# Attention beside a mixer on one core: which PSUM bank the value products and the output products take in each cycle

## The chip, the cores and the metric

The kernel runs on one core of a Trainium2 chip. The metric is the device time of one execution in microseconds (us). Before the change three runs gave 950.87, 950.03 and 948.76 us, with a median of 950.03 us.

## What is computed

The input `x` has 2048 tokens of 448 features, in float32. Two branches are computed and mixed token by token with a gate `g`:

```python
q = (x @ wq).reshape(B, S, 16, 28).transpose(0, 2, 1, 3)     # 16 heads of 28
k = x @ wk; v = x @ wv                                        # one head of keys and values, shared
p = softmax(einsum("bhqd,bkd->bhqk", q, k) * 28 ** -0.5)
a = einsum("bhqk,bkd->bhqd", p, v).transpose(0, 2, 1, 3).reshape(B, S, 448) @ wo
h = gelu(layernorm(x) @ w1)           # its four quarters shifted by +1, -1, +2, -2 tokens
x1 = x + shifted(h) @ w2
b = x1 + gelu(layernorm(x1) @ w3) @ w4
out = g * a + (1 - g) * b             # g = sigmoid(sum(x * gate_w))
```

## The kernel before

The program has three stages. The first (to about 125 us) makes queries, keys, values and the token mixer; the second (to about 400 us) is the mixer's MLP; the third, from about 400 us to the end, is attention with the output projection. The change lies in the third stage alone. The order of the instructions on TensorE, VectorE, ScalarE and SyncE is written out by hand; each engine runs its instructions in the order in which the code issues them, with semaphores between the engines.

The third stage goes through 16 units (`u`), one for each block of 512 tokens and each group of four heads. A unit has eight cycles (`i` from 0 to 7), so there are 128 cycles (`c`). A cycle handles two tiles of 128 keys, A and B:

- `scores` (line 203): twelve matmuls for a tile, in three rounds of four. The four heads of a round run side by side on four strips of 32 rows, each into its own PSUM bank: two single banks and the two halves of a pair.
- `exps` (line 850): ScalarE's exponentials of the scores, into an SBUF tile `p`. The two single banks are read one at a time (128x512), the pair of tile B at once (128x1024, `p<-pair`). The pair of tile A is first moved to SBUF by VectorE (line 888, `p<-pair`, COPY), and ScalarE then works on it in place (`p<-p`).
- `values` (line 861): eight products of `p` with the values, for the two tiles of the cycle before, all accumulated in one single bank (column strips of 32). VectorE adds that bank to the unit's sum `o` with `values_end` (line 787; line 785 for a unit's first cycle).
- `run_jobs`: output products of an earlier unit in halves of 224 columns (line 813 on TensorE, `wo_products`), followed by VectorE's addition to the output tile (line 832, `wo_add`; line 844 for a last part of the MLP that is done in the first cycles). Most cycles have one half, cycle `i == 5` has two, and from the fifth cycle of the last unit on each has two. In cycle `i == 2` the place is taken by `max_part` (line 210 on TensorE, a reduction of line 212 on VectorE), which serves the next unit. Six cycles, at the start of the stage and in the last unit, have nothing of the kind.

There are four single banks, `singles`. In each cycle they are named `s0, s1, s2, s3_`; in the next cycle the two halves of the list change places, so that what was `s0, s1` becomes `s2, s3_`. Tile A's first two heads go to `s0` and `s1`, tile B's to `s2` and `s3_`. When the exponentials of tile A have read `s0` and `s1`, these two take the cycle's other products: `s0` the output products, `s1` the values. In the next cycle tile B's scores go into both.

TensorE's order in a cycle is: scores A, scores B, output products, values. VectorE's is: the move of pair A, small work of the cycle (reciprocals, the normalisation, the next unit's queries), `wo_add`, `values_end`. The lines that set it:

```python
s0, s1, s2, s3_ = singles if c % 2 == 0 else singles[2:] + singles[:2]
...
run_jobs(s0, 2 if i == TWICE or (u == NU - 1 and i > 3) else 1)
...
pv = s1
values(k - 2, pv, True, False)
values(k - 1, pv, False, True)
values_end(v, pv)
```

After the last cycle comes a tail for the last unit: the last two value tiles, their addition to `o` (line 980), four transposes (line 986) into PSUM, normalisation by token (lines 947 and 951), four transposes back (line 956, `tail_back`) with ScalarE's copies (line 957), the output products of four times 128 tokens (line 813, `tail_wo`) and their additions and stores (lines 964 to 969). Between them stand a few matmuls on zeros (line 977, `keep_warm`) and the reduction of a check (lines 1000 to 1011) whose result a branch reads; the branch's other side is not taken with these inputs.

Of the kernel before, what the change touches and what calls it, by code (L numbers as in the profile page):

```python
# [16 lines left out]
P = 128  # L17
# [7 lines left out]
NT = S // P  # L25
# [16 lines left out]
def gated_mix_kernel(  # L42
# [137 lines left out]
    NU = NB * NG  # L180
# [24 lines left out]
    def max_part(u, ts, ps):  # L205
        if u not in mx_of:
            mx_of[u] = late.tile([P, 4, 4], F32, tag="mr", bufs=2, name=f"mr_{u}")
        n = len(ts)
        for i, t in enumerate(ts):
            nc.tensor.matmul(ps[:, i * 4 * MK:(i + 1) * 4 * MK], qh_of[u][:, t * P:(t + 1) * P], khd,  # L210
                             start=True, stop=True)
        nc.vector.reduce_max(mx_of[u][:, :, ts[0]:ts[0] + n].rearrange("p j t -> p t j"),
                             ps[:, 0:n * 4 * MK].rearrange("p (t j k) -> p t j k", t=n, j=4), axis=AX.X)
# [19 lines left out]
    def max_end(u):  # L233
        mr = mx_of.pop(u).rearrange("p j t -> p (j t)")
        mc = late.tile([P, 32], F32R, tag="mc", bufs=2, name=f"mc_{u}")
        nc.vector.tensor_scalar(mc[:, 0:16], mr, -1.0, None, op0=ALU.mult)
        nc.vector.scalar_tensor_tensor(mc[:, 16:32], mr, -1.0, f32(mc)[:, 0:16],
                                       op0=ALU.mult, op1=ALU.subtract)
        mrow = late.tile([P, 32], F32, tag="mrow", bufs=2, name=f"mrow_{u}")
        nc.vector.transpose(mrow, f32(mc))  # L240
        for k in range(2):
            rows = f32(qh_of[u])[DH + k:P:32, :].rearrange("j (t p q) -> p j t q", p=4, q=32)
            for p in range(4):
                nc.sync.dma_start(rows[p], mrow[32 * p + 16 * k:32 * p + 16 * k + 16, :])
# [4 lines left out]
    with tc.tile_pool(name="s1b", bufs=1) as s1b, \  # L249
            tc.tile_pool(name="ps1", bufs=1, space=PSUM) as ps1:  # L250
        s1_stack = ExitStack()
        s1 = s1_stack.enter_context(tc.tile_pool(name="s1", bufs=1))
# [491 lines left out]
    with tc.tile_pool(name="s3", bufs=1, reuse_waits="tile") as s3, \  # L744
# [4 lines left out]
        singles = [mm_tile("bank_0"), mm_tile("bank_1"), misc_tile("bank_2"), max_tile("bank_3")]  # L749
        pairs = [ps3.tile([P, 2, 512], F32, name=f"pair_{i}") for i in range(2)]  # L750
# [10 lines left out]
        def q_fetch(u):  # L761
            if u < NU:
                q_load(u, qr)

        def q_begin(u):
            q_split(u, s3.tile([P, 512], F32R, tag="qh", bufs=3, name=f"qh_{u}"),
                    s3.tile([P, 512], F32R, tag="ql", bufs=3, name=f"ql_{u}"))
# [14 lines left out]
        def values_end(u, pv):  # L782
            if u not in o_of:
                o_of[u] = s3.tile([P, 512], F32, tag="o", bufs=2, name=f"o_{u}")
                nc.vector.tensor_copy(o_of[u], pv)
            else:
                nc.vector.tensor_add(o_of[u], o_of[u], pv)  # L787
# [7 lines left out]
        def recip(u, o, rt, checked=True):  # L795
            if checked:
                check(rt.rearrange("p (a b) -> p a b", b=4), 0)
            rr = s3.tile([P, 16], F32, tag="rr", bufs=2, name=f"rr_{u}")
            nc.vector.reciprocal(rr, rt)
            rd = dram.tile([4, 512], F32, tag="rd", bufs=2, name=f"rd_{u}")  # L800
            nc.sync.dma_start(rd.rearrange("j (a b) -> (j a) b", b=16), rr)
            rb = s3.tile([P, 512], F32, tag="rb", bufs=2, name=f"rb_{u}")
            nc.sync.dma_start(rb, rd.unsqueeze(1).broadcast_to([4, 32, 512]))
            return u, o, rb

        def norm(u, o, rb):
            on_of[u] = s3.tile([P, 512], F32, tag="on", bufs=2, name=f"on_{u}")
            nc.vector.tensor_mul(on_of[u], o, rb)
# [9 lines left out]
        halves = [slice(0, D // 2), slice(D // 2, D)]  # L818
# [30 lines left out]
        def exps(p, heads, source=None):  # L849
            nc.scalar.activation(p[:, heads], p[:, heads] if source is None else source, AF.Exp, scale=SCALE)  # L850

        def score_tiles(u, kt, first, second, pair):
            scores(u, kt, [first, second, pair[:, 0], pair[:, 1]])
            p_of[u * NT + kt] = p = s3.tile([P, 4, 512], F32, tag="p", bufs=PB, name=f"p_{u}_{kt}")
            return p

        def values(k, pv, first, last):
            u, kt = divmod(k, NT)
            p = p_of.pop(k)
            for j in range(4):  # L860
                nc.tensor.matmul(pv[32 * j:32 * j + 32, :], vext[:, kt, :], p[:, j],  # L861
                                 start=first, stop=last, tile_position=(0, 32 * j))

        jobs = [(w4_products, w4_add, (t,), cols) for t in range(4) for cols in halves]
        left, right, both = slice(0, 1), slice(1, 2), slice(2, 4)
        sums, norms, later = [], [], []
        pv = None
        MAX_AT = 2
        TWICE = 5

        def run_jobs(ps, n):
            adds = []
            for _ in range(min(n, len(jobs))):
                products, add, args, cols = jobs.pop(0)
                products(*args, ps, cols)
                adds.append((add, args, cols))
            for add, args, cols in adds:
                add(*args, ps, cols)

        for c in range(NU * NT // 2 + 1):  # L880
            u, i = divmod(c, NT // 2)
            k = 2 * c
            s0, s1, s2, s3_ = singles if c % 2 == 0 else singles[2:] + singles[:2]
            if u < NU:
                pa = score_tiles(u, 2 * i, s0, s1, pairs[0])
                exps(pa, left, s0.unsqueeze(1))
                exps(pa, right, s1.unsqueeze(1))
                nc.vector.tensor_copy(pa[:, both], pairs[0])  # L888
                while later:
                    later.pop(0)()  # L890
                if i == 1 and sums:
                    norms.append(recip(*sums.pop()))
                if i == 1 and u == 0:
                    q_begin(1)
                    q_fetch(2)
                if i == 3 and norms:
                    w = norms[0][0]
                    norm(*norms.pop())
                if i == 6 and u + 2 < NU:
                    q_begin(u + 2)  # L900
                    q_fetch(u + 3)
                pb = score_tiles(u, 2 * i + 1, s2, s3_, pairs[1])
                exps(pb, left, s2.unsqueeze(1))
                exps(pb, right, s3_.unsqueeze(1))
                exps(pb, both, pairs[1])
                exps(pa, both)
                if i == 4 and u:
                    jobs += [(wo_products, wo_add, (u - 1, t), cols) for t in range(4) for cols in halves]
                if i == MAX_AT and u + 1 < NU:
                    max_part(u + 1, range(4), s0)  # L910
                    later.append(lambda u=u: max_end(u + 1))
                elif c == 0:
                    run_jobs(s0, 2)
                    run_jobs(s1, 2)
                else:
                    run_jobs(s0, 2 if i == TWICE or (u == NU - 1 and i > 3) else 1)
            if c:
                v = (c - 1) // (NT // 2)
                pv = s1
                values(k - 2, pv, True, False)  # L920
                values(k - 1, pv, False, True)
                if (v, i) != (NU - 1, 0):
                    values_end(v, pv)
                if i == 0 and v < NU - 1:
                    sums.append(sums_begin(v))
            if u == NU:
                break
        assert not sums and not norms and not jobs and not later

        u = NU - 1  # L930
# [2 lines left out]
        on = s3.tile([P, 512], F32, tag="on", bufs=2, name=f"on_{u}")  # L933
        on_of[u] = on
        toks = [slice(t * P, (t + 1) * P) for t in range(4)]
        b1, b0, b2, b3 = singles
        tp = [q.rearrange("p (t n) -> p t n", t=4) for q in (b1, b2)]
        tq = [q[:, 0:P] for q in (b3, b0, pairs[0][:, 0], pairs[1][:, 0])]
        wo_banks = [b1, b2, b3, b0]
        rr = s3.tile([P, 2, 2, 4], F32, name="rr4")  # L940
        on4 = s3.tile([P, 4, P], F32, name="on4")

# [12 lines left out]
        def tail_back(t):  # L955
            nc.tensor.transpose(tq[t], on4[:, t], ident)
            nc.scalar.copy(on[:, toks[t]], tq[t])
# [17 lines left out]
        def keep_warm(n):  # L975
            for _ in range(n):
                nc.tensor.matmul(pairs[1][:, 1, 0:256], warm[:, 0:P], warm, start=True, stop=True)
# [21 lines left out]
        worst = s3.tile([P, 1], F32, name="worst")  # L999
        nc.vector.tensor_reduce(worst, good, axis=AX.XY, op=ALU.min)  # L1000
        tail_back(2)
        keep_warm(2)
        tail_wo(0)
        tail_back(3)
        tail_wo(1)
        tw = pairs[0][0:1, 1, 0:P]
        nc.tensor.transpose(tw, worst, ident)
# [84 lines left out]
```

## Time and profile before

| | us |
|---|---|
| median of three runs | 950.03 |
| the profiled execution | 949.08 |
| its span, first to last instruction | 947.3 |
| TensorE (PE) busy | 936.6 |
| ScalarE (ACT) busy | 638.3 |
| VectorE (DVE) busy | 509.9 |
| GpSimd (POOL) busy | 80.8 |

The profile is of one execution. PE is the matmuls, PEld the loads of their stationary operand, which run ahead of the matmuls; a busy PE is not a PE at its peak, since matmuls overlap and their ends are modelled. In the lists of instructions in order of time a row gives the start, the time from the first start to the last end of the merged instructions, the engine, the line, the operation, the tile written and the tiles read, the shape, and the count; in brackets stands the engine's idle time before the row and what ended it. The granted TensorE clock is 0.998 of full speed over the span.

### The profile page before, as it was taken

How to read it: one execution, taken by the hardware profiler on the slowest of the kernel's cores; microseconds unless marked ns; L12 is line 12 of the kernel's file. 1: busy time of each engine (PE TensorE's matmuls, PEld its weight loads, DVE VectorE, ACT ScalarE, POOL GpSimd, SP SyncE). 2: the span in 40 equal slices, each digit the busy share in tenths (PEclk: the TensorE clock that was granted, in tenths of full speed). 3: DMA queues.
4: the chain of work that ended last, by engine and by line, in shares of the span. 5: the costliest groups of instructions: out<-in, count | busy, mean ns of one | idle time of the engine just before them, and what ended most of it. 6: DMA issues, size and time to landing. Idle time of an engine off the chain costs nothing.

```text
span 947.3 us, 19530 instructions
## 1 busy us (share of the span) xinstructions
PE 936.6 (99%) x8087; PEld 580.0 (61%) x8087; DVE 509.9 (54%) x830; ACT 638.3 (67%) x1006; POOL 80.8 (9%) x111
## 2 busy tenths in 40 slices
PE   9999999999999999999999999999999999999997
PEld 6788888888888888844444444444444444444442
DVE  4664464432432421265666666666666666666654
ACT  5542444322222222299999999999999999999993
POOL 3342500200000420110000000000000000000000
PEclk9999999999999999999999999999999999999999
DMA  8933452300300300010000001000010000110001
GB/s 291 303 84 76 138 167 84 94 9 1 84 1 1 84 1 1 23 38 24 12 23 14 23 32 34 24 12 23 15 50 24 14 23 12 33 44 11 6 13 43
DMA packets 40423, 47.05 MB, mean 50 GB/s; under 512 B 10120, under 2 KB 28488, under 8 KB 40328
## 3 DMA queue, kind: packets, MB, share of 16 engines
q1 hardware_dynamic: 37304, 40.27, 14.2%
q10 hardware_dynamic: 3024, 5.47, 1.6%
q8 instruction: 65, 1.06, 0.5%
q14 instruction: 30, 0.25, 0.1%
HBM read 32.56 MB, written 11.67 MB: 47 GB/s over the span
## 4 chain that ended last, share of the span: by engine, by line
PE 97%; ACT 1%; DVE 0%; DMA 0%; issue 0%; DVEq 0%
PE bank L861 24%; PE bank L203 21%; PE bank L813 7%; PE acc L682 5%; PE acc L684 5%; PE acc L683 5%; PE g L135 4%; PE g L136 4%; PE g L137 4%; PE pair L203 3%; PE hs L460 1%; PE hs L461 1%; PE g L138 1%; PE g L139 1%; PE h L135 1%; PE h L136 1%
## 5 line engine op out<-in xcount | busy, mean ns | idle before, releaser
L850 ACT ACTIVATE p<-bank 128x512 f32<-128x512 f32 x512 | 264.6, 603 | 33.0 <-PE pair L203 14.6
L861 PE MATMUL bank<-p,vext 128*32 128x512 f32 x2048 | 244.2, 593 | 1.7 <-ACT p L850 1.7
L888 DVE COPY p<-pair 128x1024 f32<-128x1024 f32 x128 | 156.7, 1224 | 23.5 <-PE pair L203 20.3
L672 ACT ACTIVATE gh<-g 128x512 fp32r<-128x512 f32 x55 | 32.9, 598 | 184.1 <-PE g L139 184.1
L203 PEld LDWEIGHTS bank<-qh,kh 32*128 32x128 f32 x512 | 70.1, 182 | 135.2 <-ACT p L850 106.0
L203 PE MATMUL bank<-qh,kh 32*128 32x512 f32 x512 | 146.4, 469 | 0.2
L850 ACT ACTIVATE p<-p 128x1024 f32<-128x1024 f32 x128 | 139.6, 1091 | 0.0
L787 DVE TENSOR_TENSOR o<-o,bank 128x512 f32<-128x512 f32 x111 | 76.3, 688 | 113.8 <-PE bank L861 96.4
L850 ACT ACTIVATE p<-pair 128x1024 f32<-128x1024 f32 x128 | 135.1, 1055 | 0.0
L203 PE MATMUL bank<-ql,kh 32*128 32x512 f32 x512 | 132.1, 395 | 0.0
L203 PE MATMUL pair<-qh,kh 32*128 32x512 f32 x512 | 128.0, 495 | 0.3 <-DVE x L738 0.3
L203 PE MATMUL bank<-qh,kl 32*128 32x512 f32 x512 | 128.2, 388 | 0.0
L674 DVE TENSOR_TENSOR gl<-gf,gh 128x512 fp32r<-128x512 f32 x55 | 38.3, 696 | 166.2 <-ACT gf L673 166.2
L861 PEld LDWEIGHTS bank<-p,vext 128*32 128x32 f32 x2048 | 57.9, 109 | 102.5 <-issue 77.1
L203 PE MATMUL pair<-qh,kl 32*128 32x512 f32 x512 | 101.2, 390 | 0.0
L203 PE MATMUL pair<-ql,kh 32*128 32x512 f32 x512 | 100.5, 387 | 0.0
L682 PE MATMUL acc<-w4h,gh 128*128 128x448 f32 x220 | 80.3, 365 | 0.0
L684 PE MATMUL acc<-w4h,gl 128*128 128x448 f32 x220 | 80.0, 364 | 0.0
L683 PE MATMUL acc<-w4l,gh 128*128 128x448 f32 x220 | 80.0, 363 | 0.0
L203 PEld LDWEIGHTS bank<-qh,kl 32*128 32x128 f32 x512 | 70.6, 183 | 7.9
L813 PE MATMUL bank<-wof,on 128*32 128x224 f32 (+1 forms) x992 | 70.2, 369 | 0.0
L135 PE MATMUL g<-ah,w3h 128*128 128x512 f32 x168 | 65.8, 392 | 0.0
(200 smaller groups left out, 1424.3 us busy)
## 6 DMA issues: line engine op xcount, KB each, us to landing
qd<-qf ACTq DMA_DIRECT2D x16, 256.0 KB
rb<-rd SPq DMA_DIRECT2D x15, 256.0 KB
x<-in_x_dram SPq DMA_DIRECT2D x4, 896.0 KB
xd<-xt SPq DMA_DIRECT2D x16, 224.0 KB
w34raw<-in_w_dram SPq DMA_DIRECT2D x7, 512.0 KB
qr<-qd SPq DMA_DIRECT2D x64, 56.0 KB
out_dram<-ot SPq DMA_DIRECT2D x15, 224.0 KB
w34raw<-in_w_dram SPq DMA_DIRECT2D x7, 448.0 KB
```

The costliest lines, as they stand in the source:

```text
L135: nc.tensor.matmul(ps, wh[:, c, :], ah[:, c, :], start=(c == 0), stop=False)
L136: nc.tensor.matmul(ps, wh[:, c, :], al[:, c, :], start=False, stop=False)
L203: nc.tensor.matmul(ps[j], k[h, keys], q[h, :], start=(r == 0), stop=(r == 2), tile_position=(32 * j, 0))
L674: nc.vector.tensor_sub(gl, gf, f32(gh))
L682: nc.tensor.matmul(ps, gh[:, tok], w4h[i][:, k, :], start=(f == 0), stop=False)
L683: nc.tensor.matmul(ps, gh[:, tok], w4l[i][:, k, :], start=False, stop=False)
L684: nc.tensor.matmul(ps, gl[:, tok], w4h[i][:, k, :], start=False, stop=(f == stop))
L787: nc.vector.tensor_add(o_of[u], o_of[u], pv)
L813: nc.tensor.matmul(ps[32 * i:32 * i + 32, :], a[:, c:c + 32], w, start=True, stop=True, tile_position=(0, 32 * i))
L850: nc.scalar.activation(p[:, heads], p[:, heads] if source is None else source, AF.Exp, scale=SCALE)
L861: nc.tensor.matmul(pv[32 * j:32 * j + 32, :], vext[:, kt, :], p[:, j], start=first, stop=last, tile_position=(0, 32 * j))
L888: nc.vector.tensor_copy(pa[:, both], pairs[0])
```

## The change

The value products now take `s0` and come directly behind scores B, with `values_end` behind them on VectorE; the output products (or `max_part`) take `s1` and come behind the values, and so do their additions on VectorE. The order of the cycle on TensorE becomes: scores A, scores B, values, output products.

In the last cycle VectorE no longer moves pair A; ScalarE reads it from PSUM as its third exponential of the cycle, ahead of tile B's. The values of the last two tiles are taken out of the loop and go into the first half of pair A instead of a single bank.

In the tail the transposes and products are spread over the four single banks in another way, the fourth transpose back comes directly behind the third, and two matmuls on zeros that stood between are gone, so that the first two output products follow one another.

```diff
-        for c in range(NU * NT // 2 + 1):
+        NC = NU * NT // 2
+        for c in range(NC):
...
+            pa = score_tiles(u, 2 * i, s0, s1, pairs[0])
+            exps(pa, left, s0.unsqueeze(1))
+            exps(pa, right, s1.unsqueeze(1))
+            if c < NC - 1:
                 nc.vector.tensor_copy(pa[:, both], pairs[0])
...
+            else:
+                exps(pa, both, pairs[0])
...
+            exps(pb, left, s2.unsqueeze(1))
+            exps(pb, right, s3_.unsqueeze(1))
+            exps(pb, both, pairs[1])
+            if c < NC - 1:
                 exps(pa, both)
...
-                    max_part(u + 1, range(4), s0)
...
-                    run_jobs(s0, 2 if i == TWICE or (u == NU - 1 and i > 3) else 1)
             if c:
                 v = (c - 1) // (NT // 2)
-                pv = s1
-                values(k - 2, pv, True, False)
-                values(k - 1, pv, False, True)
-                if (v, i) != (NU - 1, 0):
-                    values_end(v, pv)
+                values(k - 2, s0, True, False)
+                values(k - 1, s0, False, True)
+                values_end(v, s0)
...
+            if i == MAX_AT and u + 1 < NU:
+                max_part(u + 1, range(4), s1)
...
+                run_jobs(s1, 2 if i == TWICE or (u == NU - 1 and i > 3) else 1)
+        pv = pairs[0][:, 0]
+        values(2 * NC - 2, pv, True, False)
+        values(2 * NC - 1, pv, False, True)
...
-        b1, b0, b2, b3 = singles
-        tp = [q.rearrange("p (t n) -> p t n", t=4) for q in (b1, b2)]
-        tq = [q[:, 0:P] for q in (b3, b0, pairs[0][:, 0], pairs[1][:, 0])]
-        wo_banks = [b1, b2, b3, b0]
+        tp = [q.rearrange("p (t n) -> p t n", t=4) for q in singles[:2]]
+        tq = [singles[2 + t % 2][:, t // 2 * P:t // 2 * P + P] for t in range(4)]
+        wo_banks = singles
...
         tail_back(2)
-        keep_warm(2)
+        tail_back(3)
         tail_wo(0)
-        tail_back(3)
         tail_wo(1)
```

More of the change, by code (lines that the diff above doesn't have):

```diff
@@ L883, in gated_mix_kernel @@
             s0, s1, s2, s3_ = singles if c % 2 == 0 else singles[2:] + singles[:2]
[L884 to L887, printed above, removed]
+            pa = score_tiles(u, 2 * i, s0, s1, pairs[0])
+            exps(pa, left, s0.unsqueeze(1))
+            exps(pa, right, s1.unsqueeze(1))
+            if c < NC - 1:
                 nc.vector.tensor_copy(pa[:, both], pairs[0])
[L889 to L905, printed above, removed]
-                exps(pa, both)
-                if i == 4 and u:
-                    jobs += [(wo_products, wo_add, (u - 1, t), cols) for t in range(4) for cols in halves]
-                if i == MAX_AT and u + 1 < NU:
-                    max_part(u + 1, range(4), s0)
[L911 to L915, printed above, removed]
-                    run_jobs(s0, 2 if i == TWICE or (u == NU - 1 and i > 3) else 1)
@@ new lines, in gated_mix_kernel @@
+            else:
+                exps(pa, both, pairs[0])
+            while later:
+                later.pop(0)()
+            if i == 1 and sums:
+                norms.append(recip(*sums.pop()))
+            if i == 1 and u == 0:
+                q_begin(1)
+                q_fetch(2)
+            if i == 3 and norms:
+                w = norms[0][0]
+                norm(*norms.pop())
+            if i == 6 and u + 2 < NU:
+                q_begin(u + 2)
+                q_fetch(u + 3)
+            pb = score_tiles(u, 2 * i + 1, s2, s3_, pairs[1])
@@ L924, in gated_mix_kernel @@
                 if i == 0 and v < NU - 1:
                     sums.append(sums_begin(v))
-            if u == NU:
-                break
+            if i == 4 and u:
+                jobs += [(wo_products, wo_add, (u - 1, t), cols) for t in range(4) for cols in halves]
+            if i == MAX_AT and u + 1 < NU:
+                max_part(u + 1, range(4), s1)
+                later.append(lambda u=u: max_end(u + 1))
+            elif c == 0:
+                run_jobs(s0, 2)
+                run_jobs(s1, 2)
+            else:
+                run_jobs(s1, 2 if i == TWICE or (u == NU - 1 and i > 3) else 1)
```

## The prediction

> **What bounds the kernel now.** I read the page first, then the waits inside the attention stage (440 to 930 us), then single cycles in order of time, engine by engine.
>
> ```profile
> PE 936.6 (99%) x8087; PEld 580.0 (61%) x8087; DVE 509.9 (54%) x830; ACT 638.3 (67%) x1006; POOL 80.8 (9%) x111
> ...
> L850 ACT ACTIVATE p<-bank 128x512 f32<-128x512 f32 x512 | 264.6, 603 | 33.0 <-PE pair L203 14.6
> ```
> ```profile
> PEld bank L203 <- DVE o L787: 19.7, 103, 0.5
> ```
>
> TensorE is never without work, so a gain must come out of its own stream. The wait that the change touches is that of the score loads for VectorE's sum (L787): 103 times, 19.7 us in all, 0.19 each. A cycle with one output product shows what it does. These are the weight loads, then VectorE, then ScalarE:
>
> ```profile
> 893.95 0.18 PEld L203 LDWEIGHTS bank<-qh,kh 32*128 32x128 f32 x1 [0.18 <-DVE o L787]
> ...
> 894.85 0.16 PEld L813 LDWEIGHTS bank<-wof,on 128*32 128x32 f32 x8 [0.36 <-ACT p L850]
> ...
> 897.08 0.18 PEld L203 LDWEIGHTS bank<-qh,kh 32*128 32x128 f32 x2 [0.84 <-ACT p L850]
> ...
> 897.65 0.18 PEld L203 LDWEIGHTS bank<-qh,kh 32*128 32x128 f32 x1
> 898.02 0.18 PEld L203 LDWEIGHTS bank<-qh,kh 32*128 32x128 f32 x1 [0.18 <-DVE o L787]
> ```
> ```profile
> 895.57 0.45 DVE L832 SCALAR_TENSOR_TENSOR ot<-bank,gg,ot 128x224 f32<-128x224 f32 x1 [0.27 <-PE bank L813]
> 897.28 0.69 DVE L787 TENSOR_TENSOR o<-o,bank 128x512 f32<-128x512 f32 x1 [1.25 <-PE bank L861]
> ```
> ```profile
> 894.06 2.07 ACT L850 ACTIVATE p<-bank 128x512 f32<-128x512 f32 x4
> ```
>
> Tile B's first load stands at 897.65. Its second, for the bank that the values had, waits until L787 ends at 897.97 and comes at 898.02, 0.05 behind it. From that held load to the first product load is 0.90 us (893.95 to 894.85), and from there to the next held load 3.17 us: 4.07 us, the cycle. So a cycle is the loop "products, VectorE reads the last bank, scores B, products". ScalarE is not in it yet: the first of four exponentials takes 0.60 (603 ns in the page's row) and starts at 894.06, so it would let the product loads go at about 894.71, 0.14 before they do. More than 0.14 us per cycle can't be won here.
>
> **One product, 88 cycles.** The change turns the order round. What values alone take is seen in a cycle without products:
>
> ```profile
> 433.24 0.18 PEld L203 LDWEIGHTS bank<-qh,kh 32*128 32x128 f32 x1 [0.18 <-DVE o L787]
> ...
> 434.50 0.16 PEld L861 LDWEIGHTS bank<-p,vext 128*32 128x32 f32 x8 [0.73 <-ACT p L850]
> ...
> 436.35 0.18 PEld L203 LDWEIGHTS bank<-qh,kh 32*128 32x128 f32 x2 [0.84 <-ACT p L850]
> ...
> 437.29 0.18 PEld L203 LDWEIGHTS bank<-qh,kh 32*128 32x128 f32 x1 [0.17 <-DVE o L787]
> ```
> ```profile
> 436.55 0.69 DVE L787 TENSOR_TENSOR o<-o,bank 128x512 f32<-128x512 f32 x1 [1.95 <-PE bank L861]
> ```
>
> From the first load of the values to the next scores 1.85 us, and the sum starts 2.05 us after that first load, 0.20 behind the score load. Laid on the cycle above: values loaded at 894.85, sum from 896.90 to 897.59, which is 0.38 earlier than before. The product adds 0.38 us behind the values (2.23 from 894.85 to 897.08, less 1.85), so the next scores still load at 897.08, and with the same lag of 0.20 VectorE may have the product at 897.28. It is then still at the sum: the addition L832, which stood ahead of the sum, is now queued behind it, and tile B's second load waits for the addition. What an addition costs directly behind a long operation shows elsewhere:
>
> ```profile
> 592.86 0.69 DVE L195 TENSOR_TENSOR ql<-qr,qh 128x512 fp32r<-128x512 f32 x1
> 593.47 0.44 DVE L832 SCALAR_TENSOR_TENSOR ot<-bank,gg,x 128x224 f32<-128x224 f32 x1
> ```
> ```profile
> 572.31 0.36 DVE L832 SCALAR_TENSOR_TENSOR ot<-bank,gg,ot 128x224 f32<-128x224 f32 x1
> ```
>
> L832 starts 0.08 before the end of the operation ahead of it (593.55) and takes 0.44; behind a reciprocal of 16 elements it took 0.36. With the first row, which has an operation of the sum's kind and size ahead, it runs from 897.51 to 897.95 and the load comes at 898.00: 0.02 earlier than before, 88 times, 1.8 us gained. Bounds: with 0.36 it is 0.10 earlier (8.8 us gained), without the overlap 0.06 later (5.3 us lost). I take 0.02.
>
> The Trainium skill's page "VectorE: DVE Perf Modes", section "The DRAIN you can't avoid", speaks against this change: the next operation does not start until the pipe of the one before is empty. By that rule the sum would come out at the lossy end; the two rows at 592.86 and 593.47 show an earlier start, so I give the measurement the greater weight.
>
> **Two products, 17 cycles that have a cycle behind them** (the fifth-index cycle of 15 units, and two more of the last).
>
> ```profile
> 587.58 0.54 PEld L813 LDWEIGHTS bank<-wof,on 128*32 128x32 f32 x16 [0.36 <-ACT p L850]
> ...
> 590.19 0.18 PEld L203 LDWEIGHTS bank<-qh,kh 32*128 32x128 f32 x2 [0.84 <-ACT p L850]
> ...
> 591.13 0.18 PEld L203 LDWEIGHTS bank<-qh,kh 32*128 32x128 f32 x1 [0.18 <-DVE o L787]
> ```
> ```profile
> 588.68 0.81 DVE L832 SCALAR_TENSOR_TENSOR ot<-bank,gg,x 128x224 f32<-128x224 f32 x2 [0.65 <-PE bank L813]
> ```
>
> The first addition starts 1.10 us behind the first product load, so it waits for both products. Now the sum runs from 589.63 to 590.32, the products are ready at 590.19 + 0.20 = 590.39, and VectorE stands idle for 0.07 before them. The two additions end at 591.20, the load comes at 591.25 instead of 591.13. That is 0.12 later; as the lag of 0.20 was read behind values, I take 0.13: 17 x 0.13 = 2.2 us lost.
>
> **The next unit's maximum, 15 cycles.**
>
> ```profile
> 575.16 0.52 PEld L210 LDWEIGHTS bank<-khd,qh 128*128 128x128 f32 x4 [0.36 <-ACT p L850]
> ...
> 577.61 0.18 PEld L203 LDWEIGHTS bank<-qh,kh 32*128 32x128 f32 x2 [0.84 <-ACT p L850]
> ...
> 578.54 0.18 PEld L203 LDWEIGHTS bank<-qh,kh 32*128 32x128 f32 x1 [0.18 <-DVE o L787]
> ```
> ```profile
> 575.93 0.69 DVE L212 TENSOR_REDUCE mr<-bank 128x16 f32<-128x512 f32 x1 [0.33 <-ACT p L850]
> ```
>
> The sum would run from 577.21 to 577.90, the reduction (ready at 577.81) from 577.82 to 578.51, the load at 578.56: 0.02 later, 0.3 us lost in all.
>
> **No product, 6 cycles.** Here the values start at 434.50 because they wait for the second exponential's bank; the loop would let them go 0.90 behind 433.24, at 434.14, so the first bank saves 0.36 us, and nothing is written into the second, so the following scores are not held at all. What is late next is ScalarE:
>
> ```profile
> 403.73 1.09 ACT L850 ACTIVATE p<-p 128x1024 f32<-128x1024 f32 x1
> 404.68 2.10 ACT L850 ACTIVATE p<-bank 128x512 f32<-128x512 f32 x4
> 406.59 1.11 ACT L850 ACTIVATE p<-pair 128x1024 f32<-128x1024 f32 x1
> 407.49 1.14 ACT L850 ACTIVATE p<-p 128x1024 f32<-128x1024 f32 x1
> ```
>
> Its steps here are 0.95, 1.91 and 0.90, 3.76 us in all against a cycle of 4.05 (433.24 to 437.29). A saving between 0.29 and 0.36, and a little more in the cycles behind: 6 x 0.33 = 2.0 us gained (1.7 to 2.2).
>
> **The last cycle and the tail.**
>
> ```profile
> 928.49 0.54 PEld L813 LDWEIGHTS bank<-wof,on 128*32 128x32 f32 x16 [0.36 <-ACT p L850]
> ...
> 931.69 0.28 PEld L861 LDWEIGHTS bank<-p,vext 128*32 128x32 f32 x8 [0.58 <-ACT p L850]
> ...
> 936.31 0.16 PEld L813 LDWEIGHTS bank<-wof,on 128*32 128x32 f32 x8 [0.21 <-issue]
> 937.20 0.14 PEld L956 LDWEIGHTS pair<-ident,on 128*128 128x128 f32 x1 [0.73 <-issue]
> 937.46 0.16 PEld L813 LDWEIGHTS bank<-wof,on 128*32 128x32 f32 x8
> ```
> ```profile
> 933.70 0.88 DVE L980 TENSOR_TENSOR oo<-o,bank 128x128 f32<-128x128 f32 x4 [1.72 <-PE bank L861]
> ```
>
> Before, the last products waited 0.58 us at 931.69 for ScalarE's very last exponential, tile A's. Now that one is third and tile B's last one ends at about the same time, but only half of one of the last two tiles needs it. TensorE then runs through: values and two products take 2.61 us (587.58 to 590.19) with a change of tile shape at their end, so the last values load near 931.0 and VectorE's L980 starts at 931.0 + 2.05 = 933.0 instead of 933.70: 0.7 us gained. VectorE's move in that cycle was beside other work and saves nothing itself. In the tail the two output products no longer have a transpose (0.26 us, 937.20 to 937.46) and its two changes of shape between them; the fourth transpose now waits for VectorE ahead of the first product, about where the two dropped matmuls ran. I take 0.3 us (0.1 to 0.4).
>
> **The sum.** -1.8 + 2.2 + 0.3 - 2.0 - 0.7 - 0.3 = -2.3 us on an execution of 949.08 us (span 947.3), which gives 946.8. That execution lies 0.95 us under the median of 950.03; on the median's scale the forecast is **947.7 us**, 0.24% less. About 0.2% (1.9 us) is what a measurement of this kernel tells from no change.
>
> **The rivals.**
>
> *VectorE's operations don't overlap (slower).* Place: the addition behind the sum, in the 88 cycles with one product and the 15 with a maximum. Each loses the 0.08: +0.06 x 88 = 5.3 and +0.10 x 15 = 1.5, with 2.2 for two products and -3.0 for the rest: +6.0, 956.0 us. It decides from 0.05 us on: (2.3 + 1.9) / 88. For it speaks that no row of before shows an addition behind L787; against it the row at 593.47. Chance 0.12. The page's rule named above is this rival.
>
> *The addition is short (faster).* If it takes 0.36 behind the sum, 88 x 0.08 = 7.0 us more are gained: 940.7 us. Only a very short operation stood ahead of it where it was so. Chance 0.10.
>
> *The cycles without products don't shrink.* If ScalarE, or the move of pair A behind it, sets those six cycles already, 2.0 us are missing: 949.7 us, no change. Its rows leave 0.29 us per cycle, so chance 0.10.
>
> **How the numbers follow.** The forecast has the remaining 0.68. It lies 0.4 us past the bound of 1.9, and an error of 0.01 us per cycle moves it by about 1, so I give 0.40 of it to faster and 0.28 to no change. Faster 0.40 + 0.10 = 0.50, same 0.28 + 0.10 = 0.38, slower 0.12. The range from 943.0 to 952.5 leaves out the far ends of the first two rivals, about 0.1 on either side.
>
> **What would show it.** Right: the score loads now wait for L832 and no longer for L787, with about the same sum (near 20 us) in the waits; from the first load behind the scores to the next held load 3.15 us with one product (3.17 now) and 3.68 with two (3.55 now, 587.58 to 591.13), and the cycles without any at 3.8; L980's idle time behind TensorE, and the 0.58 us at the last values, gone. Wrong: waits of the score loads well under 15 us or over 25 us, additions that start at or behind the end of L787, or a stretch of 3.55 as before in the cycles with two products.

## The result, and the profile after

The changed kernel took 947.22 us (median of 12 runs, 946.89 to 948.89) and the kernel before 949.54 us (median of 12 runs beside it, 948.76 to 950.88). The ratio is 0.9976, with a 95% interval of 0.9967 to 0.9985: 2.3 us faster, where 2.3 had been forecast. The difference is small and the agreement of the totals says little by itself, so the steps are looked at one by one.

The page, then a row of the waits between 440 and 930 us:

```profile
span 945.1 us, 19526 instructions
...
PE 936.3 (99%) x8085; PEld 585.7 (62%) x8085; DVE 504.1 (53%) x829; ACT 637.3 (67%) x1006; POOL 80.8 (9%) x111
```
```profile
PEld bank L203 <- DVE ot L832: 19.6, 99, 0.3
```

TensorE's busy time is nearly what it was. The wait for the sum (L787, 19.7 us, 103 times) is replaced by a wait for the addition (L832, 19.6 us, 99 times); behind a maximum the loads now wait for the reduction L212 (2.6 us, 14 times). The wait has changed its name and about kept its size.

**One product.** Weight loads of the changed kernel in order of time, then VectorE (start, duration, then the idle time ahead of the row and what ended it):

```profile
893.67 0.16 PEld L861 LDWEIGHTS bank<-p,vext 128*32 128x32 f32 x8 [0.36 <-ACT p L850]
...
894.98 0.13 PEld L813 LDWEIGHTS bank<-wof,on 128*32 128x32 f32 x4 [0.30 <-ACT p L850]
...
895.90 0.19 PEld L203 LDWEIGHTS bank<-qh,kh 32*128 32x128 f32 x2 [0.36 <-ACT p L850]
...
896.82 0.18 PEld L203 LDWEIGHTS bank<-qh,kh 32*128 32x128 f32 x1
...
897.71 0.16 PEld L861 LDWEIGHTS bank<-p,vext 128*32 128x32 f32 x8 [0.37 <-ACT p L850]
```
```profile
895.72 0.69 DVE L787 TENSOR_TENSOR o<-o,bank 128x512 f32<-128x512 f32 x1 [1.57 <-PE bank L861]
896.32 0.44 DVE L832 SCALAR_TENSOR_TENSOR ot<-bank,gg,ot 128x224 f32<-128x224 f32 x1
```

The sum starts 2.05 us behind the first load of the values and ends at 896.41. The addition starts 0.09 before that, ends at 896.76, and the held load comes at 896.82 (its idle time is 0.15 us, too short for the view to print). From the first load behind the scores to the held load it is 3.15 us, as forecast.

**Two products.** The same views of the cycle with two, and the held load of the cycle behind it:

```profile
585.81 0.16 PEld L861 LDWEIGHTS bank<-p,vext 128*32 128x32 f32 x8 [0.36 <-ACT p L850]
...
588.42 0.18 PEld L203 LDWEIGHTS bank<-qh,kh 32*128 32x128 f32 x2 [0.36 <-ACT p L850]
...
589.49 0.18 PEld L203 LDWEIGHTS bank<-qh,kh 32*128 32x128 f32 x1 [0.31 <-DVE ot L832]
...
593.56 0.18 PEld L203 LDWEIGHTS bank<-qh,kh 32*128 32x128 f32 x1 [0.18 <-DVE ot L832]
```
```profile
587.86 0.69 DVE L787 TENSOR_TENSOR o<-o,bank 128x512 f32<-128x512 f32 x1 [1.56 <-PE bank L861]
588.63 0.81 DVE L832 SCALAR_TENSOR_TENSOR ot<-bank,gg,x 128x224 f32<-128x224 f32 x2
```

VectorE is idle for 0.08 between the end of the sum (588.55) and the additions, which wait for the products. The held load comes 3.68 behind the first one; before it was 3.55. The cycle behind it, from 589.49 to 593.56, takes the usual 4.07.

**The next unit's maximum.** Weight loads, then VectorE:

```profile
573.42 0.16 PEld L861 LDWEIGHTS bank<-p,vext 128*32 128x32 f32 x8 [0.38 <-ACT p L850]
...
576.81 0.18 PEld L203 LDWEIGHTS bank<-qh,kh 32*128 32x128 f32 x1 [0.18 <-DVE mr L212]
```
```profile
575.47 0.69 DVE L787 TENSOR_TENSOR o<-o,bank 128x512 f32<-128x512 f32 x1 [1.59 <-PE bank L861]
576.07 0.68 DVE L212 TENSOR_REDUCE mr<-bank 128x16 f32<-128x512 f32 x1
```

3.39 us, where it was 3.38 (575.16 to 578.54).

**No product.** Weight loads, VectorE and ScalarE:

```profile
432.23 0.18 PEld L203 LDWEIGHTS bank<-qh,kh 32*128 32x128 f32 x2 [0.40 <-DVE o L787]
...
433.24 0.16 PEld L861 LDWEIGHTS bank<-p,vext 128*32 128x32 f32 x8 [0.47 <-ACT p L850]
...
436.03 0.18 PEld L203 LDWEIGHTS bank<-qh,kh 32*128 32x128 f32 x2 [0.40 <-DVE o L787]
```
```profile
435.29 0.69 DVE L787 TENSOR_TENSOR o<-o,bank 128x512 f32<-128x512 f32 x1 [1.71 <-PE bank L861]
```
```profile
432.51 2.15 ACT L850 ACTIVATE p<-bank 128x512 f32<-128x512 f32 x4
434.42 1.16 ACT L850 ACTIVATE p<-pair 128x1024 f32<-128x1024 f32 x1
435.33 1.20 ACT L850 ACTIVATE p<-p 128x1024 f32<-128x1024 f32 x1
436.27 2.20 ACT L850 ACTIVATE p<-bank 128x512 f32<-128x512 f32 x4
```

The cycle takes 3.80 us instead of 4.05. ScalarE starts each step before the recorded end of the one ahead; its steps of 1.91, 0.91 and 0.94 make 3.76 of the 3.80.

**The last cycle and the tail.** The last held load, the last values, the last sum, and the last transposes back with the first products behind them; the last held load of the kernel before stands at the end:

```profile
926.40 0.18 PEld L203 LDWEIGHTS bank<-qh,kh 32*128 32x128 f32 x1 [0.31 <-DVE ot L832]
...
929.62 0.32 PEld L861 LDWEIGHTS pair<-p,vext 128*32 128x32 f32 x8
...
934.08 0.33 PEld L958 LDWEIGHTS bank<-ident,on 128*128 128x128 f32 x2 [0.24 <-ACT on L959]
934.54 0.16 PEld L813 LDWEIGHTS bank<-wof,on 128*32 128x32 f32 x8
```
```profile
931.83 0.88 DVE L982 TENSOR_TENSOR oo<-o,pair 128x128 f32<-128x128 f32 x4 [0.89 <-issue]
```
```profile
927.59 0.18 PEld L203 LDWEIGHTS bank<-qh,kh 32*128 32x128 f32 x1 [0.18 <-DVE o L787]
```

The row at 929.62 shows no idle time: the 0.58 us ahead of the last values is gone. The idle time of VectorE ahead of the last sum (L980 before, L982 now) is not gone, as the prediction's sign had it, but fell from 1.72 to 0.89.

### The profile page after: what moved, and what is told of

It reads as the page before. It is cut to its first block, busy times and chain, and to the rows that moved or that the text cites. A ratio compares the mean times of both kernels' runs of the same rounds, so it can differ in the third digit from the quotient of the medians.

```text
span 945.1 us, 19526 instructions
## 1 busy us (share of the span) xinstructions
PE 936.3 (99%) x8085; PEld 585.7 (62%) x8085; DVE 504.1 (53%) x829; ACT 637.3 (67%) x1006; POOL 80.8 (9%) x111
## 4 chain that ended last, share of the span: by engine, by line
PE 97%; ACT 1%; DMA 0%; DVE 0%; issue 0%; DVEq 0%
PE bank L861 24%; PE bank L203 22%; PE bank L813 5%; PE acc L682 5%; PE acc L684 5%; PE acc L683 5%; PE g L135 4%; PE g L136 4%; PE g L137 4%; PE pair L203 3%; PE hs L460 1%; PE hs L461 1%; PE g L138 1%; PE g L139 1%; ACT p L850 1%; PE h L135 1%
## 5 line engine op out<-in xcount | busy, mean ns | idle before, releaser
L787 DVE TENSOR_TENSOR o<-o,bank 128x512 f32<-128x512 f32 x111 | 76.3, 687 | 149.0 <-PE bank L861 135.1
L861 PEld LDWEIGHTS bank<-p,vext 128*32 128x32 f32 x2032 | 53.0, 109 | 122.5 <-issue 76.0
L813 PEld LDWEIGHTS bank<-wof,on 128*32 128x32 f32 x992 | 32.0, 110 | 64.4 <-issue 32.1
L813 PE MATMUL bank<-wof,on 128*32 128x224 f32 (+1 forms) x992 | 67.5, 359 | 0.0
```

The lines of the kernel that those rows point to most:

```text
L813: nc.tensor.matmul(ps[32 * i:32 * i + 32, :], a[:, c:c + 32], w, start=True, stop=True, tile_position=(0, 32 * i))
```

## The experiments

Theory A is that of the prediction: in nearly all cycles the stream is held by VectorE's two operations in a row, sum and addition, whichever comes first, so exchanging them brings next to nothing; what is gained comes from the cycles without products and from the end. Its test is to make one of these operations short. The other theories stand in the expectations. The cycle lengths below are taken from one move of pair A to the next and stand in the order `i` = 0 to 7, for a unit without a disturbed cycle.

**The loop's order alone** (`loop_only`; last cycle and tail as before):

```diff
-            if c < NC - 1:
-                nc.vector.tensor_copy(pa[:, both], pairs[0])
-            else:
-                exps(pa, both, pairs[0])
+            nc.vector.tensor_copy(pa[:, both], pairs[0])
...
-            if c < NC - 1:
-                exps(pa, both)
+            exps(pa, both)
...
-        pv = pairs[0][:, 0]
+        pv = singles[1]
...
```

> The loop's new order alone; last cycle and tail as before. Theory A (VectorE's last read of the two banks sets the cycle; what the values gain by coming first is given back by the addition queued behind them, two-product cycles lose, only the six cycles without products gain): 1.0 to 1.6 us faster than before, with 6 x 0.33 gained and 16 or 17 x 0.13 lost inside. Rival B (all cycles gain a little because the new order suits TensorE): nearly the whole 2.3 us, and no cycle longer than before. Rival C (the gain sits in the last cycle and the tail): no change.

Measured: 948.32 us, ratio 0.9988 (0.9979 to 0.9997), 1.2 us faster.

**The last cycle and the tail alone** (`ends_only`; the loop's order as before):

```diff
-            if c:
...
-                values(k - 2, s0, True, False)
...
-                max_part(u + 1, range(4), s1)
+                max_part(u + 1, range(4), s0)
...
-                run_jobs(s1, 2 if i == TWICE or (u == NU - 1 and i > 3) else 1)
+                run_jobs(s0, 2 if i == TWICE or (u == NU - 1 and i > 3) else 1)
+            if c:
...
+                values(k - 2, s1, True, False)
...
```

> The new last cycle and tail alone; the loop in its order of before. Theory A: 1.0 us faster than before (0.7 in the last cycle, 0.3 in the tail). Rival B: 0 to 0.3 us. Rival C: 2.3 us.

Measured: 948.49 us, ratio 0.9986 (0.9977 to 0.9995), 1.05 us faster. The two parts add up to the whole: half of the gain comes from one cycle in 128 and the tail.

**Two products ahead of the values** (`mixed`), beside **the changed kernel again** (`after_again`):

```diff
+            two = len(jobs) > 1 and c and (i == TWICE or (u == NU - 1 and i > 3))
+            pv = s0
+            if two:
+                run_jobs(s0, 2)
+                pv = s1
             if c:
...
-                values(k - 2, s0, True, False)
...
+                values(k - 2, pv, True, False)
+                values(k - 1, pv, False, True)
...
+            elif not two:
+                run_jobs(s1, 1)
```

> As the changed kernel, but in the 18 cycles with two products these come ahead of the values and take the first bank, as before. Theory A: the loss of 0.13 to 0.14 us in 17 of them goes, so 2.2 us faster than the changed kernel, 4.5 us faster than before. Rival B: 17 of 128 cycles lose their share of the gain, 0.3 us slower than the changed kernel.

> The changed kernel, on the same chip as the parts: 2.3 us faster than before.

Measured: `mixed` 945.70 us, ratio 0.9956 (0.9942 to 0.9969); `after_again` 947.52 us, 0.9977 (0.9968 to 0.9987). Putting the old order back where there are two products is worth 1.8 us, where 2.2 were expected. Counted from move to move it shows in the cycle behind: 4.06 us instead of 4.19 in the median. The moves at the two ends of such a cycle, in `mixed` and in the changed kernel:

```profile
590.05 1.23 DVE L889 COPY p<-pair 128x1024 f32<-128x1024 f32 x1 [0.19 <-PE pair L203]
...
594.12 1.22 DVE L889 COPY p<-pair 128x1024 f32<-128x1024 f32 x1 [0.19 <-PE pair L203]
```
```profile
589.50 1.23 DVE L889 COPY p<-pair 128x1024 f32<-128x1024 f32 x1
...
593.69 1.22 DVE L889 COPY p<-pair 128x1024 f32<-128x1024 f32 x1 [0.18 <-PE pair L203]
```

**Short additions** (`short_add`). The additions leave out most columns, each reads `x1` instead of the running tile, and `x1` is what is stored:

```diff
-            before = x1[:, n, :] if g == 0 else ot_of[n]
+            before = x1[:, n, :]
...
-            nc.vector.scalar_tensor_tensor(ot_of[n][:, cols], ps[:, cols], gg[:, n:n + 1], before[:, cols],
+            few = slice(cols.start, cols.start + 8)
+            nc.vector.scalar_tensor_tensor(ot_of[n][:, few], ps[:, few], gg[:, n:n + 1], before[:, few],
...
-                nc.sync.dma_start(out[0, n * P:(n + 1) * P, :], ot_of[n])
+                nc.sync.dma_start(out[0, n * P:(n + 1) * P, :], x1[:, n, :])
```

> The changed kernel, with the loop's additions of the output products cut from 224 to 8 columns (the other columns are left out, and the tiles stored are not the sums). TensorE does the same work. Theory A: the addition then ends about 0.25 us earlier, before tile B's scores want the bank, so no score load is held in cycles with one product, and the first exponential becomes the limit at about 3.93 us in place of 4.06: 88 x 0.12 = 10.6 us, and with two products some 16 x 0.25 = 4 us: 12 to 15 us faster than the changed kernel, 933 to 936 us. Rival D (VectorE's reads don't set the cycle; drains between tile shapes or the exponentials do): within 1 us of the changed kernel.

Measured: 933.88 us, ratio 0.9836 (0.9821 to 0.9852). TensorE has the same work, and the time is in the range that was expected (933 to 936). Rows of a cycle:

```profile
895.52 0.30 PEld L203 LDWEIGHTS bank<-qh,kh 32*128 32x128 f32 x2
...
896.65 0.16 PEld L862 LDWEIGHTS bank<-p,vext 128*32 128x32 f32 x8 [0.47 <-ACT p L851]
```
```profile
894.76 0.69 DVE L787 TENSOR_TENSOR o<-o,bank 128x512 f32<-128x512 f32 x1 [1.46 <-PE bank L862]
895.37 0.22 DVE L833 SCALAR_TENSOR_TENSOR ot<-bank,gg,x 128x8 f32<-128x8 f32 x1
```

The addition is done at 895.59, and both score loads of tile B's round come together, at 895.52 and 895.64. A cycle with one product takes 3.94 us instead of 4.05. The next bound stands at 896.65: the values wait for the first exponential. This agrees with theory A: the length of the addition is on the path.

**Short sums in the order of before** (`short_sum`):

```diff
-                nc.vector.tensor_add(o_of[u], o_of[u], pv)
+                nc.vector.tensor_add(o_of[u][:, 0:8], o_of[u][:, 0:8], pv[:, 0:8])
```

> The kernel before, with the sum of the values cut to 8 of 512 columns in seven of a unit's eight cycles (the other columns are left out). Theory A: the order before was held by the sum, so it gains what the changed kernel gains from a short addition: 112 x 0.12 = 13 us, 935 to 938 us. Rival D: no change.

Measured: 945.28 us, ratio 0.9957 (0.9942 to 0.9972): 4 us faster where 13 were expected, a miss. A cycle with one product went from 4.07 to 4.05 only, and one with two from 4.45 to 4.31: some 0.02 x 88 and 0.15 x 17, which makes the 4 us. Rows of a cycle with one:

```profile
894.51 0.16 PEld L813 LDWEIGHTS bank<-wof,on 128*32 128x32 f32 x8 [0.47 <-ACT p L850]
895.00 0.16 PEld L861 LDWEIGHTS bank<-p,vext 128*32 128x32 f32 x8 [0.33 <-ACT p L850]
...
896.86 0.18 PEld L203 LDWEIGHTS bank<-qh,kh 32*128 32x128 f32 x2 [0.84 <-ACT p L850]
...
897.43 0.19 PEld L203 LDWEIGHTS bank<-qh,kh 32*128 32x128 f32 x2
```
```profile
897.05 0.16 DVE L787 TENSOR_TENSOR o<-o,bank 128x8 f32<-128x8 f32 x1 [1.36 <-PE bank L861]
```

The sum ends at 897.21 and the hold is gone: both loads come at 897.43. But with the product ahead the values go into the second bank, and that is free only when the second exponential has read it. The same two loads in the kernel before, and the start of the two exponentials in each kernel (before, then `short_sum`):

```profile
894.85 0.16 PEld L813 LDWEIGHTS bank<-wof,on 128*32 128x32 f32 x8 [0.36 <-ACT p L850]
895.20 0.18 PEld L861 LDWEIGHTS bank<-p,vext 128*32 128x32 f32 x8 [0.19 <-ACT p L850]
```
```profile
894.06 2.07 ACT L850 ACTIVATE p<-bank 128x512 f32<-128x512 f32 x4
```
```profile
893.87 2.06 ACT L850 ACTIVATE p<-bank 128x512 f32<-128x512 f32 x4
```

In `short_sum` the product's load comes 0.64 us behind the start of the exponentials instead of 0.79, but the values keep their distance from that start: 1.13 us (893.87 to 895.00), where before it was 1.14 (894.06 to 895.20). They are now 0.49 behind the product's load instead of 0.35. So for cycles with one product theory A tells only half of the order of before: there is a second bound, within 0.01 us in these rows and 0.02 us in the cycle. This is read from the rows; no run took that bound away alone. The new order doesn't have it: its values wait for the first exponential alone.

**Values in two halves of the columns** (`split`): each half goes into its own bank, with a half-sum behind it, and the product goes into the bank that is summed first. With two products, one comes ahead of the values and one behind.

```diff
+            va, vb = (s1, s0) if two else (s0, s1)
+            if two:
+                run_jobs(s0, 1)
...
-                values(k - 2, s0, True, False)
-                values(k - 1, s0, False, True)
-                values_end(v, s0)
+                value_half(k - 2, va, 0)
+                value_half(k - 2, vb, 1)
...
-                run_jobs(s1, 2 if i == TWICE or (u == NU - 1 and i > 3) else 1)
+                run_jobs(va, 1)
```

> The changed kernel with the values' 512 query columns in two halves, the first into the first bank, the second into the second, each summed by itself; the output product goes into the first bank behind them, once its half is summed. With two products the first comes ahead of the values and the second behind. All work is done, with 32 value matmuls of 256 columns in place of 16 of 512 and two sums in place of one. Theory A: VectorE's last sum and the addition end before tile B's scores want their banks, so no load is held but behind a maximum (0.08): one product 3.93 us instead of 4.06 (88 x 0.12 = 10.6), two products 4.31 instead of 4.58 (16 x 0.27 = 4.3), maximum 15 x 0.1 = 1.5: 14 to 17 us faster than the changed kernel, 930 to 933 us. Rival D: the doubled count of value matmuls costs and nothing is won: 947 us or more.

Measured: 945.79 us, ratio 0.9958 (0.9944 to 0.9971), a miss (930 to 933 were expected). Plain cycles with one product take 3.95 us, near the 3.93 expected, but those with other small work of VectorE in them don't: 4.31 at `i` = 3, 4.26 at `i` = 6, 4.44 at `i` = 5, and 5.60 in the second cycle of all.

**The halves in some cycles only** (`split_some`): from the fourth cycle on, where one product or none follows; two products as in `mixed`, values whole beside the maximum (`top`).

```diff
+                if two or top or c < 3:
+                    values(k - 2, pv, True, False)
+                    values(k - 1, pv, False, True)
+                    values_end(v, pv)
+                else:
+                    value_half(k - 2, s0, 0)
+                    value_half(k - 2, s1, 1)
...
+            elif not two:
+                run_jobs(s0, 1)
```

> The values split over the two banks only in cycles with one product or none, from the fourth cycle on; cycles with two products have them ahead of the values, in the first bank, and cycles with a maximum have it behind unsplit values, in the second bank, as in the changed kernel. All work is done. Theory A: a cycle that follows a split one starts its scores unheld and runs at 3.95 us as in the kernel with all values split (4.05 to 4.07 before), about 4.32 if it has two products and 4.16 with a maximum; a cycle behind two products or a maximum keeps 4.06. A unit of eight cycles takes about 32.4 us in place of 33.15, so some 10 us less than the kernel with two products ahead (945.7): 934 to 938 us. Rival D (the doubled value matmuls eat what the hold gives back, as the small gain of the fully split kernel may say): 943 us or more.

Measured: 943.54 us, ratio 0.9934 (0.9921 to 0.9948), a miss: theory A expected 934 to 938, and the time alone would fit rival D. The cycles tell them apart. A unit takes 3.95, 3.95, 4.15, 4.31, 3.95, 4.32, 4.26 and 3.95 us. Behind a split cycle they have the 3.95, 4.15 and 4.32 of theory A, so the doubled count of value matmuls is not what makes the loss; too long are only `i` = 3 and 6, where 4.06 was expected. What makes the fourth long is seen in a second profile of the same kernel (`split_some_again`), weight loads and VectorE:

```profile
580.52 0.16 PEld L813 LDWEIGHTS bank<-wof,on 128*32 128x32 f32 x8 [0.49 <-DVE o L877]
...
581.04 0.18 PEld L203 LDWEIGHTS bank<-qh,kh 32*128 32x128 f32 x2 [0.36 <-ACT p L850]
```
```profile
579.49 0.65 DVE L808 TENSOR_TENSOR on<-o,rb 128x512 f32<-128x512 f32 x1
580.06 0.41 DVE L877 TENSOR_TENSOR o<-o,bank 128x256 f32<-128x256 f32 x1
```

VectorE is at the normalisation (L808) until 580.14, the first half-sum stands behind it, and the product, which goes into that bank, waits 0.49 us for the half-sum; in a plain cycle it waits 0.22.

**Without the halves at `i` = 3 and 6** (`split_fewer`), to test that reading, beside `split_some` again; the edit is shown against `split_some`:

```diff
-                if two or top or c < 3:
+                if two or top or c < 3 or i in (3, 6):
...
-            elif c < 3:
+            elif c < 3 or (not two and i in (3, 6)):
                 run_jobs(s1, 1)
```

> split_some with the values unsplit, as in the changed kernel, in the fourth and the seventh cycle of every unit (i = 3 and 6); those are the cycles in which split_some took 4.31 and 4.26 us. If they are long because VectorE's small work for the next unit stands ahead of the first half-sum, and a product in the first bank has to wait for that half-sum, then both fall to about 4.06 us, while the cycles behind them (3.95) rise to about 4.06, as their score loads are held by the addition again: 0.24 + 0.20 - 2 x 0.11 = 0.22 us per unit, 16 units, about 3.5 us under split_some: about 940. If the length comes from the small work itself, wherever the product stands, the two cycles stay near 4.25 and nothing is gained, or up to 3 us lost: 943 to 947.

> The same kernel as split_some, timed beside split_fewer: 941.5 to 945 by every theory.

Measured: `split_fewer` 941.36 us, ratio 0.9913 (0.9899 to 0.9926), the fastest of those that do the whole work; `split_some_again` 943.88 us, 0.9929 (0.9916 to 0.9943). A unit takes 3.95, 3.95, 4.15, 4.07, 4.08, 4.32, 4.06 and 4.08 us: each of the four cycles (`i` = 3, 4, 6 and 7) moved as the first of the two readings said. The medians differ by 2.5 us, a little under the 3.5 expected, and the two intervals overlap; the cycles, not the times, carry the verdict.

**No output products in the loop** (`no_products`):

```diff
-        jobs = [(w4_products, w4_add, (t,), cols) for t in range(4) for cols in halves]
+        jobs = []
...
-            if i == 4 and u:
-                jobs += [(wo_products, wo_add, (u - 1, t), cols) for t in range(4) for cols in halves]
+            if i == 4 and u and (u - 1) % NG == NG - 1:
...
+                    nc.sync.dma_start(out[0, n * P:(n + 1) * P, :], x1[:, n, :])
```

> The changed kernel without any output product or late MLP product in the loop (they and their additions are left out; the tiles stored are not the sums). Theory A: every cycle but those with a maximum is like the six without products, and ScalarE sets it: 3.76 to 3.81 us, so 88 x 0.26 + 18 x 0.75 = 36 us faster, about 911 us. Rival E (the six cycles shrank for another reason, the bank alone, and a long run of such cycles is set by TensorE): 3.67 to 3.70 us per cycle, some 10 us less again.

Measured: 911.38 us, ratio 0.9609 (0.9594 to 0.9624), the 911 of theory A. Behind the first two, cycles take 3.69 to 3.83 us, as the six cycles without products do in the changed kernel, and 4.41 with a maximum. From one cycle's exponentials to the next, in a cycle without it:

```profile
701.72 2.22 ACT L850 ACTIVATE p<-bank 128x512 f32<-128x512 f32 x4
...
705.49 2.27 ACT L850 ACTIVATE p<-bank 128x512 f32<-128x512 f32 x4
```

That is 3.77 us without idle time. From 440 to 880 us ScalarE waits 3.2 us in all, where in the changed kernel it waits 24.2, so ScalarE sets these cycles.

## Why the prediction was right

Its steps, with the lengths of all cycles added up by kind in the two profiles (us, after less before). A cycle is counted here from one held load to the next, as the prediction counts it, so that a late load falls into the cycle that makes it late.

| step | forecast | profile | worked out |
|---|---|---|---|
| one product | -1.8 | -1.7 | 88 cycles, 359.2 to 357.5; the median cycle is 0.015 shorter |
| two products | +2.2 | +2.3 | 17 cycles, 75.5 to 77.8; the median cycle is 0.137 longer |
| maximum | +0.3 | +0.2 | 15 cycles, 64.2 to 64.4; the median cycle is 0.008 longer |
| no product | -2.0 | -1.9 | 6 cycles, 24.3 to 22.4 |
| last cycle | -0.7 | -0.7 | last held load to last sum: 6.11 (927.59 to 933.70) to 5.43 (926.40 to 931.83) |
| tail | -0.3 | -0.3 | last sum to the end: 13.57 to 13.30 |

The sum of the column is -2.1; the spans differ by 2.2, since the first held load too comes 0.15 us earlier (400.42 to 400.28), and the medians by 2.3. No step failed, and each has its forecast sign and size, but the sizes are finer than the profiles carry: 0.01 us in a hundred cycles is 1 us. In a second profile of the changed kernel (`after_again`) the row of one product comes to -1.1, mostly because its second cycle alone is 0.44 longer.

The last cycle met its size by two deviations that cancel. The last values load 3.22 us behind the held load and not 3.41, and the last sum starts 2.21 behind them and not 2.05. In the tail the first output product comes 0.10 us later behind the last sum, and from it to the check's transpose 0.40 less passes (2.04 to 1.64). That the forecast met the difference to 0.1 us is partly luck.

Three statements were wrong without harm to the sum. TensorE was said to be never without work. But its matmuls, 8085 in either case, are busy for 936.3 us in the changed kernel and for 918.9 in `short_add`, so a busy share of 99% has waiting in it. Of the kernel before it was said that ScalarE is not in the loop and that 0.14 us per cycle is the most to be won; that bound was taken from the first exponential, while the values of before go by the second, with 0.01 to 0.02 us to spare (`short_sum`). It did not show, since the new order moves the values to the first. And in the cycles without a product the scores were to be "not held at all". They are held for 0.40 us by the sum (436.03), but ScalarE has no gap then, so it costs nothing.

The rivals:
- *VectorE's operations don't overlap.* The addition starts 0.08 to 0.09 us before the recorded end of the sum in 86 of the 88 cycles with one product; in the other two, disturbed ones, it starts 0.06 behind it. The reduction of the maximum starts 0.08 to 0.09 us before that end in all 15 (576.07 against 576.16). With no overlap the time would have been 956.0. The Trainium skill's page "VectorE: DVE Perf Modes", section "The DRAIN you can't avoid", says that the next operation does not start until the pipe is empty, and adds that one which is not held starts earlier. The prediction took the first sentence alone, so it was wrong to count the page against the change; the rows go with the second.
- *The addition is short.* It took 0.44 to 0.45 us behind the sum, as the row at 593.47 had it, and not 0.36.
- *The cycles without products don't shrink.* From move to move they went from 4.05 to between 3.67 and 3.81.

`short_add` shows why the exchange alone brings so little. The 0.38 us by which the sum comes earlier are used up by the addition behind it (0.35 from the end of the sum to the end of the addition). Take most of its length out, and the ratio falls from 0.9977 to 0.9836, about 13 us.

## What to carry to other kernels

When a wait ends at the last of several operations in a row on one engine, changing their order may only rename the wait, as here (19.7 us to 19.6). What moved it in these runs was a shorter operation (`short_add`) or a bank released in parts (`split_fewer`). Before counting on a wait that is to go, look for the next one within a few hundredths of a microsecond: here each order had its own next bound, the second exponential in one and the first in the other, so the worth of a shorter sum or addition depended on the order. And place a step by what already stands on its engine in that cycle: the same halved sum gained 0.1 us in plain cycles and lost 0.2 where VectorE had small work ahead of it.

## What the runs showed that was not expected

- Some cycles are 0.1 to 0.4 us longer than others of their kind, at places that recur: the fifth cycle of the fourth unit and the first of the seventh are 0.35 longer in the kernel before and 0.14 in both profiles of the changed kernel, and the fifth of the ninth is 0.37 longer in the changed kernel and not in the kernel before. The cause was not studied.
- The attention stage began (first move of pair A) at 400.9 to 401.8 us in ten of the profiles and at 403.2 to 403.6 in three, those of `split` and (twice) `split_some`, although the stages before it are the same in the code. The delay arises at the very start: the twenty-first matmul of the program begins at 8.8 to 9.0 us in these three and at 6.7 to 7.7 in the others. The cause is open. So some 2 us of the misses of `split` and `split_some` may have nothing to do with the change, and times of single profiles are not compared across kernels here to better than 3 us.
